# Running both score units of a key block back to back, with the AV output in the FFN's PSUM ring

## The chip, the cores and the metric

The kernel runs on one core of a Trainium2 chip. The metric is the device time of one execution in microseconds (us); each version was executed several times, and medians are given. A run can contain stretches of 3.4 us in which TensorE gets half its clock.

Names: PE is TensorE, DVE is VectorE, ACT is ScalarE, POOL is GpSimd. The kernel uses PSUM, where TensorE writes its results, as eight banks of 128 x 512 fp32 values.

## The reference, cut to what matters

Attention with a sliding window and four sink tokens, then RMS normalisation and a SwiGLU FFN:

```python
scores = scale * np.matmul(q, k.transpose(0, 1, 3, 2))       # q, k, v: 4 x 8 heads x 768 x 64
keep = is_sink | in_window                                   # 4 sinks, window of 128
a = softmax(np.where(keep, scores, -1e9))
x = (a @ v) transposed to 3072 x 512
xn = x / rms(x) * rms_g
g, val = xn @ w_gate, xn @ w_val                             # 512 -> 1536
out = (g * sigmoid(g) * val) @ w_out                         # 1536 -> 512, fp32
```

The kernel cuts the 3072 rows into 24 key blocks of 128 and, for the FFN, into 6 groups of 4 blocks.

## The kernel before

TensorE executes in the order of the program text. ScalarE's and VectorE's order in the main part is chosen at build time. All semaphores are made automatically: a tile taken from a pool waits until the last reader of the tile that had that buffer before is done. Tiles of one tag form a ring: with `bufs=4`, most tiles wait for the one four tiles earlier. (Which bank a tile gets is fixed at build time. In the kernel after, rebuilt to check this, about three reuses in four are at that distance; the others are from two to seven tiles back.)

The PSUM banks of the main part: four for the tag `b1` (gate `pg`, value `pvl`, output `po`, transposes `pqk` and `pxt`, sink tiles `pss` and `pvs`), two for `pT` (one slot of two banks), two for `pv`.

```python
# ... (pools)
pp[0] = ctx.enter_context(tc.tile_pool(name="psum", bufs=4, space=bass.MemoryType.PSUM))

def unit_s(g, u):                    # scores of 4 heads of key block g
    # ...
    pT = pp[0].tile([P, 2, 512], FP32, name="pT", tag="pT", bufs=1)
    for j in range(2):
        hp = 2 * u + j
        for hi in range(2):
            pr = slice(hi * D, (hi + 1) * D)         # 64 of the 128 rows of the array
            nc.tensor.matmul(out=pT[:, hi, j * 256:j * 256 + w],
                lhsT=QKT[b][pr, 1, hp, t * P:(t + 1) * P],
                rhs=QKT[b][pr, 0, hp, t * P:t * P + w], start=True, stop=True)      # L366
    et = epool.tile([P, 4, 2, P], BF16, name="et")
    nc.scalar.activation(out=et[...], in_=pT[...], func=ACT.Exp, scale=inv_sqrt_d)  # L373
    # ... mask: one DVE product (L386), or two POOL selects for later blocks (L388, L393)

def unit_av(g, u):                   # A times V of 4 heads, with the softmax sum as 65th column
    pv = pp[0].tile([P, 512], FP32, name="pv", tag="b1" if PROLOGUE[0] else "pv", bufs=2)
    # ... 4 to 9 short matmuls, then reciprocal (L449) and scaling (L454) on DVE,
    # sum of squares on ACT (L464); after u == 1 the normalisation chain on DVE (L473 to L511)

def parts_f(G, fts, cols):           # two parts of the FFN: gate and value
    def gate():                      # 4 matmuls of 512 columns into pg, then
        # ... th = tanh(pg / 2) on ACT (L564)
    def val():                       # 4 matmuls into pvl, then
        # ... p1 = (th + 1) * pg on DVE (L569): pg's bank is free
        # ... hT = p1 * pvl on DVE (L577): pvl's bank is free
# parts_o: 12 matmuls into po in three parts (L592), then osb = po / 2 on ACT (L599), DMA out

def step(g):                         # the attention work of block g in four slots
    slots = [[], [], [], []]
    if g < NB:
        slots[0].append(lambda: unit_s(g, 0))
        slots[2].append(lambda: unit_s(g, 1))
        # ... sink units in slot 1
    if g <= NB:
        slots[1].append(lambda: unit_av(g - 1, 0))
        slots[3].append(lambda: unit_av(g - 1, 1))
    # ... transposes of x in slot 0, of q and k in slots 1 or 2
    return slots
# weave(): the slots are spread evenly between the FFN's parts
```

The softmax here doesn't subtract the row's maximum and nothing guards it: scores larger than these inputs give would overflow.

## Time and profile before

| | before |
|---|---|
| time, median of 4 runs beside the change | 262.55 us (262.2 to 262.65) |
| TensorE busy | 93% |
| VectorE, ScalarE, GpSimd busy | 68%, 53%, 37% |
| TensorE waits of the profiled run after 38 us | 4.2 us |

These are lines of the page of the kernel before: busy time and share, then the span in 40 slices of 6.6 us (a digit is the busy share in tenths), the clock that TensorE was granted, and the chain of work that ended last.

```profile
...
PE 244.9 (93%) x1735; PEld 125.7 (48%) x1762; DVE 178.9 (68%) x471; ACT 137.9 (53%) x277; POOL 98.4 (37%) x131
...
PE   5878969989999999999999997999999999999994
...
DVE  3566866798768999438899449799338894078800
...
PEclk9999997999999999999999999999999999999998
...
PE 76%; DMA 10%; ACT 4%; DVE 4%; POOL 3%; issue 2%; POOLq 0%; ACTq 0%
...
```

From the seventh slice on TensorE has nine tenths or more almost everywhere: it is the limit, and 76% of the chain is its work. But VectorE has stretches of 8s and 9s too (the ninth, the thirteenth to the sixteenth, and so on): these are the gate/value stretches of the FFN groups. There is little room behind TensorE.

From the groups view, the three large groups of matmuls. After the bar: busy us, mean ns of one, then the us for which TensorE sat idle just before them, and for whom.

```profile
...
L551 PE MATMUL pg<-xnt,wg 128*128 128x512 bf16 (+1 forms) x321 | 74.4, 356 | 2.6 <-DVE p_2594 L569 1.7
L551 PE MATMUL pvl<-xnt,wv 128*128 128x512 bf16 (+1 forms) x319 | 74.0, 356 | 0.9 <-ACT xnt L537 0.5
L592 PE MATMUL po<-wo,hT 128*128 128x512 bf16 x278 | 65.7, 379 | 0.5
...
```

And from the waits view of TensorE: who waited for whom, us in total, times, longest.

```profile
...
PE pg L551 <- DVE p_2594 L569: 1.7, 1, 1.7
PE pT L366 <- ACT qkT L263: 1.4, 2, 0.9
PE pT L366 <- ACT qkT L241: 1.3, 2, 0.7
...
PE pvl L551 <- ACT xnt L537: 0.5, 1, 0.5
...
```

Past the start-up there is one long wait: 1.7 us, a gate tile whose bank was held until VectorE's product L569 was done. No line has a score unit waiting for an exponential to free `pT`.

The timeline of TensorE around one score unit shows why one wants to bring the two units together (start us, length us, line, count; the length runs to the modelled end of the last matmul):

```profile
...
102.26 1.03 PE L551 MATMUL pvl<-xnt,wv 128*128 128x512 bf16 x4
103.22 0.39 PE L366 MATMUL pT<-qkT 64*128 64x256 bf16 x4
103.54 1.90 PE L592 MATMUL po<-wo,hT 128*128 128x512 bf16 x8
...
```

Gate and value matmuls of 512 columns follow each other every 0.216 us. Four value matmuls started at 102.26 make the next start due at 103.12. The score unit starts at 103.22, 0.10 us late. The output matmul comes 0.32 us after it. The two matmuls of a pair use different halves of the rows and run together (they start 3 to 4 ns apart), so the visit is two pairs of 256 columns. The Trainium skill ("TensorEngine Tiling (Array Packing)", Key Properties) says that a change of tiling mode drains TensorE; this trace agrees.

### The profile page before, as it was taken

What the parts mean: (1) busy time and instruction counts of PE and PEld (TensorE: products, weight loads), DVE (VectorE), ACT (ScalarE), POOL (GpSimd) and SP (SyncE); (2) the same over time, 40 slices, a digit from 0 to 9 for tenths busy, and PEclk for the clock granted to TensorE, in tenths of its full rate; (3) what the DMA queues carried; (4) which work ended last, traced back from release to release, by engine and by line L of the source; (5) the groups of instructions that cost most, each with busy time, mean ns of one, the idle gap of its engine ahead of it and who ended that gap; (6) DMA issues with size and microseconds to landing.
All of it is one profiled execution on the core that took longest, in us unless ns stands there. A gap on an engine that the chain in (4) does not pass through costs nothing.

```text
span 262.4 us, 4760 instructions
## 1 busy us (share of the span) xinstructions
PE 244.9 (93%) x1735; PEld 125.7 (48%) x1762; DVE 178.9 (68%) x471; ACT 137.9 (53%) x277; POOL 98.4 (37%) x131
## 2 busy tenths in 40 slices
PE   5878969989999999999999997999999999999994
PEld 2446757845454444444454443444444454444441
DVE  3566866798768999438899449799338894078800
ACT  2646755687786546456465554464654542233211
POOL 8997679299988340413112001114112000000000
PEclk9999997999999999999999999999999999999998
DMA  9999999999999999441112450411330112300022
GB/s 98 138 173 182 187 163 186 185 155 149 170 178 181 147 134 130 105 149 30 22 21 42 116 148 16 62 21 40 102 101 1 22 20 60 114 8 0 0 82 80
DMA packets 105991, 25.74 MB, mean 98 GB/s; under 512 B 95088, under 2 KB 102768, under 8 KB 105968
## 3 DMA queue, kind: packets, MB, share of 16 engines
q0 software_dynamic: 82784, 14.16, 75.5%
q1 hardware_dynamic: 23184, 11.28, 18.8%
q8 instruction: 14, 0.23, 0.4%
q14 instruction: 9, 0.07, 0.1%
HBM read 28.57 MB, written 6.29 MB: 133 GB/s over the span
## 4 chain that ended last, share of the span: by engine, by line
PE 76%; DMA 10%; ACT 4%; DVE 4%; POOL 3%; issue 2%; POOLq 0%; ACTq 0%
PE pg L551 22%; PE pvl L551 21%; PE po L592 21%; PE pT L366 4%; DMA qs<-in_q_dram 4%; DMA wg<-in_moe_w_gate_dram 3%; DMA wv<-in_moe_w_val_dram 3%; PE pv L426 2%; ACT et L373 1%; PE pv L422 1%; PE pqk L228 1%; PE pv L414 1%; PE pss L298 1%; POOL qs L111 1%; ACT sq L464 1%
## 5 line engine op out<-in xcount | busy, mean ns | idle before, releaser
L551 PE MATMUL pg<-xnt,wg 128*128 128x512 bf16 (+1 forms) x321 | 74.4, 356 | 2.6 <-DVE p_2594 L569 1.7
L551 PE MATMUL pvl<-xnt,wv 128*128 128x512 bf16 (+1 forms) x319 | 74.0, 356 | 0.9 <-ACT xnt L537 0.5
L592 PE MATMUL po<-wo,hT 128*128 128x512 bf16 x278 | 65.7, 379 | 0.5
L564 ACT ACTIVATE th<-pg 128x512 bf16<-128x512 f32 x72 | 42.7, 594 | 42.1 <-PE pg L551 41.4
L388 POOL TENSOR_SCALAR_AFFINE_SELECT et<-et 128x512 bf16<-128x512 bf16 x20 | 12.8, 638 | 87.2 <-ACT et L373 71.7
L373 ACT ACTIVATE et<-pT 128x1024 bf16<-128x1024 f32 (+1 forms) x42 | 39.4, 937 | 10.2 <-PE pT L366 10.2
L551 PEld LDWEIGHTS <-wv 128*128 128x128 bf16 x328 | 30.5, 99 | 28.2 <-issue 2.3
L551 PEld LDWEIGHTS <-wg 128*128 128x128 bf16 x328 | 30.1, 98 | 28.6 <-issue 4.0
L592 PEld LDWEIGHTS <-hT 128*128 128x128 bf16 x288 | 26.4, 98 | 29.5 <-issue 1.5
L599 ACT ACTIVATE osb<-po 128x512 f32<-128x512 f32 x24 | 14.3, 595 | 28.3 <-PE po L592 24.3
L111 POOL DMA_DIRECT2D qs<-in_q_dram x24 | 21.5, 897 | 9.3 <-DMA wo<-in_moe_w_out_dram 2.6
L111 POOL DMA_DIRECT2D ks<-in_k_dram x24 | 21.4, 892 | 7.8 <-PE pg L551 2.7
L449 DVE RECIPROCAL rden<-pv 128x4 f32<-128x4 f32 x48 | 8.4, 176 | 19.7 <-PE pv L426 19.7
L366 PE MATMUL pT<-qkT 64*128 64x256 bf16 (+1 forms) x168 | 15.8, 267 | 2.9 <-ACT qkT L263 1.4
L386 DVE TENSOR_TENSOR et<-et,masks 128x1024 bf16<-128x1024 bf16 (+1 forms) x22 | 14.1, 640 | 5.7 <-ACT et L373 5.5
L366 PEld LDWEIGHTS <-qkT 64*128 64x128 bf16 x168 | 5.3, 94 | 18.7 <-issue 18.3
L426 PEld LDWEIGHTS <-et 128*128 128x128 bf16 x168 | 11.6, 97 | 1.6
L422 PEld LDWEIGHTS <-et 128*128 128x128 bf16 x136 | 10.8, 98 | 3.1
L393 POOL TENSOR_SCALAR_AFFINE_SELECT et<-et 128x512 bf16<-128x512 bf16 x16 | 11.1, 692 | 0.0
L414 PE MATMUL pv<-vsk,esk 128*128 128x260 bf16 x32 | 8.8, 274 | 0.0
L263 ACT COPY qkT<-pqk 128x1024 bf16<-128x1024 bf16 x8 | 8.1, 1007 | 0.9 <-PE pqk L228 0.9
L228 PE MATMUL pqk<-ident,qs 128*128 128x128 bf16 x56 | 5.5, 221 | 2.8 <-DMA qs<-in_q_dram 2.8
(318 smaller groups left out, 341.8 us busy)
## 6 DMA issues: line engine op xcount, KB each, us to landing
out_dram<-osb SPq DMA_DIRECT2D x24, 256.0 KB, 2.2
qs<-in_q_dram POOLq DMA_DIRECT2D x24, 128.0 KB, 7.4
ks<-in_k_dram POOLq DMA_DIRECT2D x24, 128.0 KB, 7.5
wg<-in_moe_w_gate_dram POOLq DMA_DIRECT2D x6, 256.0 KB, 7.6
wv<-in_moe_w_val_dram POOLq DMA_DIRECT2D x6, 256.0 KB, 8.0
wo<-in_moe_w_out_dram POOLq DMA_DIRECT2D x2, 768.0 KB, 11.0
v_100<-in_v_dram POOLq DMA_DIRECT2D x6, 128.0 KB, 7.8
v_102<-in_v_dram POOLq DMA_DIRECT2D x6, 128.0 KB, 7.7
```

Source lines behind the costliest of these rows:

```text
L111: nc.gpsimd.dma_start(out=tl, in_=src[b, :, t * P:(t + 1) * P, :].rearrange("h t d -> t h d"),)
L366: nc.tensor.matmul(out=pT[:, hi, j * 256:j * 256 + w], lhsT=QKT[b][pr, 1, hp, t * P:(t + 1) * P], rhs=QKT[b][pr, 0, hp, t * P:t * P + w], ...
L373: nc.scalar.activation(out=et[:, :, 0:nq, :].rearrange("p x n c -> p x (n c)"), in_=pT.rearrange("p i (j c) -> p (i j) c", c=256)[:, :, 0: ...
L386: nc.vector.tensor_tensor(out=ev, in0=ev, in1=mv, op=ALU.mult)
L388: nc.gpsimd.affine_select(out=et[:, :, 0, :], in_=et[:, :, 0, :], compare_op=ALU.is_ge, fill=0.0, base=0, pattern=[[0, 4], [1, P]], channe ...
L414: nc.tensor.matmul(out=pv[:, 0:HW], lhsT=ESK[(b, t)], rhs=VSK[b][:, 4 * u:4 * u + 4, :], start=True, stop=False, skip_group_check=True,)
L422: nc.tensor.matmul(out=dest, lhsT=E[(g - 1, h, 1)], rhs=V16[b][:, t - 1, h, :], start=(t == 1), stop=False, skip_group_check=True,)
L426: nc.tensor.matmul(out=dest, lhsT=E[(g, h, 0)], rhs=V16[b][:, t, h, :], start=(t == 0), stop=True, skip_group_check=True,)
L551: nc.tensor.matmul(out=ps[:, i * n:(i + 1) * n], lhsT=w_sb[:, kt, ft * P:(ft + 1) * P], rhs=XNT[G][:, kt, cols], start=(kt == 0), stop=(kt ...
L564: nc.scalar.activation(out=st["th"], in_=st["pg"], func=ACT.Tanh, scale=0.5)
L592: nc.tensor.matmul(out=st["po"], lhsT=HT[(G, ft // 2)][:, ft % 2, tb * P:(tb + 1) * P], rhs=wo[:, ft, :], start=(ft == 0), stop=(ft == FTN ...
L599: nc.scalar.mul(osb, st["po"], 0.5)
```

## The change

The intent: run the two score units of a block as one visit of eight matmuls. Each needs its own PSUM slot then, or the second would wait for the exponential of the first. The second slot takes two banks, and these are the two that AV had; AV goes into the ring of four with everything else. The diff, cut to its core:

```diff
@@ unit_bias, unit_s
-        pT = pp[0].tile([P, 2, 512], FP32, name="pT", tag="pT", bufs=1)
+        pT = pp[0].tile([P, 2, 512], FP32, name="pT", tag="pT", bufs=2)
@@ unit_av
-            [P, 512], FP32, name="pv", tag="b1" if PROLOGUE[0] else "pv", bufs=2
+            [P, 512], FP32, name="pv", tag="b1"
@@ step
             slots[0].append(lambda: unit_s(g, 0))
-            slots[2].append(lambda: unit_s(g, 1))
+            slots[0].append(lambda: unit_s(g, 1))
...
-            slots[0].append(lambda: unit_x(g - 3))
+            slots[0].insert(0, lambda: unit_x(g - 3))
@@ (the first two unit_x are taken out of their slots, as before)
-        slots[6].pop()
-        slots[10].pop()
+        slots[6].pop(0)
+        slots[10].pop(0)
```

The step function makes blocks 5 to 23, so 19 blocks are paired.

More of the change, by code (lines that the diff above doesn't have):

```diff
@@ L360, in unit_s @@
         w = nq * P
-        pT = pp[0].tile([P, 2, 512], FP32, name="pT", tag="pT", bufs=1)
+        pT = pp[0].tile([P, 2, 512], FP32, name="pT", tag="pT", bufs=2)
         for j in range(2):
```

## The prediction

> **What bounds it now.** Up to about 38 us the kernel waits for loads (slice view: DMA 9 of ten). From there TensorE is the limit: it is 93% busy over the span, and the chain of waits is 76% PE, 10% DMA, 4% ACT, 4% DVE. The groups view shows few PE waits: 2.6 us before pg, 0.9 before pvl, 2.9 before pT. A second limit lies close behind: in the gate/value stretches the windows view has VectorE busy 94% (78-103 us), 88% (118-142) and 86% (154-181), and the longest late wait, 1.68 us at 162 us, is a gate matmul whose bank waits for VectorE's product (L569).
>
> **What the change saves.** Score units use 64 rows of the array, their neighbours 128. The Trainium skill ("TensorEngine Tiling (Array Packing)", Key Properties) says that a change of tiling mode drains TensorE. The timeline agrees: value matmuls start every 0.216 us from 102.26, so the next start is due at 103.12; the score unit starts at 103.22 (0.10 late), and the next matmul 0.32 us after it, though two pairs of 256 columns need 0.213. A visit costs about 0.21 us beyond its work. In 19 blocks (5 to 23) two visits become one: at most 19 x 0.21 = 4.0 us. The second pT slot itself saves almost nothing: the waits view has no PE wait for an exponential (L373) to free pT.
>
> **What it costs.** Two AV tiles a block join the ring of four banks that holds gate, value, output, transposes and sink tiles. pg is free only after tanh (0.59 us) and product (0.66), pvl after another 0.69, pv after reciprocal and scaling (0.17 + 0.42), each behind queues. I laid the recorded bank releases against the tile order with AV included: if releases stay put while TensorE slips, 2 to 3.5 us of stalls appear; if they slip along entirely, 13. Tightest: 58-74 us, where units come at every part and an output tile's bank waits for its scaled copy (L599) behind exponentials and copies; then 125-139, 162 and 174 us, where VectorE is behind. Estimate between: 4 us.
>
> The two exponentials (1.02 us each) now come together, so a tanh behind them is up to 1 us later; in blocks below 12 the two mask products (0.68 each) come together too. Where an AV tile is among the next three ring tiles, this reaches the gate bank: estimate 0.5 us. And where VectorE is full, perhaps 0.5 us of TensorE's saving is lost.
>
> **Sum.** Gain 4.0; costs 4 + 0.5 + 0.5 = 5. All lies past 38 us on the critical path. Net +1 us: **263.5 us**, 8 times in 10 between 259.2 and 268.5. Faster by over 2%: 0.05; within 2%: 0.78; slower by over 2%: 0.17.
>
> **What the profile would show.** Right: pT matmuls in runs of eight, with one entry gap of 0.10 us and one exit of 0.11 a block; new PE waits before pg, pvl, po and pv, on VectorE (L569, L577, L454) and ScalarE (L599), 4-6 us more than before, most at 55-78 us and in the late gate/value stretches; no new wait before pT; start-up and the last stretch (from 217 us) unchanged in length. Wrong: no new waits, then about 258.6 us; or waits over 9 us, then slower by over 2%.
>
> **What would make it wrong.** ScalarE's and VectorE's order is chosen anew at build time: it may put tanh and products ahead of exponentials and masks, and hide the stalls; or put normalisation late, so that AV tiles hold ring banks long. Adjacency may also not remove the drain.

## The result

| | before | after |
|---|---|---|
| median of 4 runs | 262.55 us | 265.89 us (265.06 to 266.77) |
| ratio | | 1.013, 95% interval 1.0093 to 1.0167 |
| profiled span | 262.4 us | 265.1 us |

A ratio here is the mean time of one kernel's runs over the mean of the other's of the same rounds, so it is not quite the ratio of the medians. The change is 1.3% slower: a loss clear of noise, but under 2%.

The same lines of the page, after:

```profile
...
PE 243.9 (92%) x1735; PEld 128.9 (49%) x1762; DVE 181.7 (69%) x471; ACT 138.1 (52%) x277; POOL 99.8 (38%) x131
...
PE   5978979978999989998999996999999999999994
...
DVE  3567868887779999439988459689329994078700
...
PEclk9999999999999999999999999799999999999999
...
PE 65%; DVE 14%; DMA 7%; POOL 6%; ACT 4%; issue 3%; POOLq 0%; ACTq 0%
...
```

TensorE's busy time fell by 1 us and the span grew by 2.7: time went into waiting. The chain shows it best: PE's share falls from 76 to 65%, VectorE's rises from 4 to 14%. VectorE's own busy share is almost what it was (69% instead of 68), with the same 471 instructions. It is waited for more, without having more to do.

The groups:

```profile
...
L551 PE MATMUL pvl<-xnt,wv 128*128 128x512 bf16 (+1 forms) x322 | 74.3, 356 | 3.3 <-DVE p L569 1.4
L551 PE MATMUL pg<-xnt,wg 128*128 128x512 bf16 (+1 forms) x317 | 74.4, 355 | 2.1 <-DVE hT L577 0.9
...
L592 PE MATMUL po<-wo,hT 128*128 128x512 bf16 x279 | 65.0, 379 | 1.1 <-DVE p L569 0.6
...
```

The idle time before value matmuls rises from 0.9 to 3.3 us and before output matmuls from 0.5 to 1.1; the AV group, which had none but a 1.0 us wait for a load at the start, now has a wait of 1.9 us. The waits view lists them (only those past the start-up are shown, and the one of `pT` for comparison):

```profile
...
PE pv L426 <- DVE p L569: 1.9, 1, 1.9
...
PE pvl L551 <- DVE p L569: 1.4, 2, 0.9
PE pT L366 <- ACT qkT L241: 1.3, 2, 0.7
...
PE pvl L551 <- DVE y L479: 0.9, 1, 0.9
PE pg L551 <- DVE hT L577: 0.9, 2, 0.7
PE pvl L551 <- DVE hT L577: 0.8, 2, 0.5
PE po L592 <- DVE p L569: 0.6, 1, 0.6
...
PE pqk L228 <- ACT osb L599: 0.3, 1, 0.3
...
```

Each line but that of `pT` is a tile that waits for a bank: for a gate product (L569), a value product (L577), an output copy (L599). "DVE y L479" names the wrong instruction: that value tile, at 58.76 us, has the bank of a sink tile, whose reader L287 ran from 58.28 to 58.70. Added over the trace past 38 us, TensorE's waits are 8.8 us, against 4.2 before; the waits for banks alone are 6.8 us against 2.2 (the gate tile's 1.7 and a value tile's 0.5, whose bank the copy L537 still read). The longest is not new: the 1.9 us of AV at 164 us wait for the same kind of product as the gate tile's 1.7 us, at the same place, in the kernel before. These idle times are still too small: the profile lets a 512-column matmul last 0.38 us while the next could start after 0.216, so each wait after such a matmul hides another 0.16 us.

One such wait in full. This is the timeline of the kernel after, on all engines, with other rows left out (start, length, engine, line, count, and in brackets idle time and releaser):

```profile
...
120.30 1.03 PE L551 MATMUL pvl<-xnt,wv 128*128 128x512 bf16 x4
...
121.26 0.61 PE L366 MATMUL pT<-qkT 64*128 64x256 bf16 x8
...
121.69 1.94 ACT L373 ACTIVATE et<-pT 128x1024 bf16<-128x1024 f32 x2 [0.18 <-PE pT L366]
...
121.80 1.04 PE L551 MATMUL pg<-xnt,wg 128*128 128x512 bf16 x4
...
122.68 1.03 PE L551 MATMUL pvl<-xnt,wv 128*128 128x512 bf16 x4
...
123.52 0.60 ACT L564 ACTIVATE th<-pg 128x512 bf16<-128x512 f32 x1
...
123.89 1.02 PE L551 MATMUL pg<-xnt,wg 128*128 128x512 bf16 x3
...
124.07 1.08 DVE L511 SCALAR_TENSOR_TENSOR xr<-x,y,gb 128x512 bf16<-128x512 bf16 x1
...
125.07 0.68 DVE L569 SCALAR_TENSOR_TENSOR p<-th,pg 128x512 bf16<-128x512 bf16 x1
...
125.80 1.02 PE L551 MATMUL pvl<-xnt,wv 128*128 128x512 bf16 x4 [0.89 <-DVE p L569]
...
```

The gain is there: value matmuls from 120.30, next start due at 121.16, eight score matmuls at 121.26, next matmul at 121.80. That is 0.10 + 0.54 us for a block, where two visits before cost 2 x (0.10 + 0.32) = 0.84: 0.20 us saved.

Then it is given back. The gate tile at 121.80 ends at 122.84. Its tanh starts at 123.52, because ScalarE has both exponentials to do first (1.94 us). Its product L569 starts only at 125.07, because VectorE's order has the block's normalisation chain ahead of it, with `xr` (L511) from 124.07 to 125.15 last. So its bank is free at 125.75. The ring since then: gate (121.80), value (122.68), AV (between 123.5 and 123.9), gate (123.89), and now the value tile that needs the first one's bank. It should start at 124.75 and starts at 125.80. Without the AV tile in the ring, the tile that reuses this bank would be the one after, due at 125.6: by this reckoning a wait of about 0.2 us instead of 1.05.

### The profile page after: what moved, and what is told of

Read it like the earlier page. It is cut to its first block, busy times and chain, and to the rows that moved or that the text cites. A ratio compares the mean times of both kernels' runs of the same rounds, so it can differ in the third digit from the quotient of the medians.

```text
span 265.1 us, 4754 instructions
## 1 busy us (share of the span) xinstructions
PE 243.9 (92%) x1735; PEld 128.9 (49%) x1762; DVE 181.7 (69%) x471; ACT 138.1 (52%) x277; POOL 99.8 (38%) x131
## 4 chain that ended last, share of the span: by engine, by line
PE 65%; DVE 14%; DMA 7%; POOL 6%; ACT 4%; issue 3%; POOLq 0%; ACTq 0%
PE po L592 23%; PE pg L551 18%; PE pvl L551 16%; DMA qs<-in_q_dram 4%; DVE p L569 4%; DMA wg<-in_moe_w_gate_dram 3%; DVE hT L577 3%; DVE xr L511 3%; PE pT L366 2%; ACT th L564 2%; POOL v L124 2%; DVE et L386 2%; ACT et L373 1%; PE pqk L228 1%; PE pv L426 1%
## 5 line engine op out<-in xcount | busy, mean ns | idle before, releaser
L564 ACT ACTIVATE th<-pg 128x512 bf16<-128x512 f32 x72 | 42.8, 595 | 51.5 <-PE pg L551 51.4
L569 DVE SCALAR_TENSOR_TENSOR p<-th,pg 128x512 bf16<-128x512 bf16 x72 | 49.2, 684 | 24.3 <-ACT th L564 23.8
L577 DVE TENSOR_TENSOR hT<-p,pvl 128x512 bf16<-128x512 bf16 x72 | 49.3, 685 | 3.9 <-DVE p L569 0.5
L388 POOL TENSOR_SCALAR_AFFINE_SELECT et<-et 128x512 bf16<-128x512 bf16 x20 | 12.6, 636 | 84.7 <-ACT et L373 62.8
L373 ACT ACTIVATE et<-pT 128x1024 bf16<-128x1024 f32 (+1 forms) x42 | 37.7, 942 | 5.7 <-PE pT L366 5.7
L464 ACT ACTIVATE sq<-x 128x256 bf16<-128x256 bf16 x48 | 19.9, 415 | 20.0 <-DVE x L454 19.7
L599 ACT ACTIVATE osb<-po 128x512 f32<-128x512 f32 x24 | 14.3, 598 | 28.1 <-PE po L592 22.4
L124 POOL DMA_DIRECT2D v<-in_v_dram x24 | 21.4, 893 | 1.7 <-DMA qs<-in_q_dram 1.0
L511 DVE SCALAR_TENSOR_TENSOR xr<-x,y,gb 128x512 bf16<-128x512 bf16 (+1 forms) x25 | 20.6, 827 | 0.6
L454 DVE TENSOR_TENSOR x<-pv,rden 128x256 bf16<-128x256 f32 x48 | 20.2, 422 | 1.0
L426 PE MATMUL pv<-v,et 128*128 128x65 bf16 x168 | 15.3, 193 | 1.9 <-DVE p L569 1.9
L386 DVE TENSOR_TENSOR et<-et,masks 128x1024 bf16<-128x1024 bf16 (+1 forms) x22 | 13.9, 639 | 3.4 <-ACT et L373 3.2
L366 PE MATMUL pT<-qkT 64*128 64x256 bf16 (+1 forms) x168 | 12.3, 262 | 1.3 <-ACT qkT L241 1.3
```

The costliest lines, as they stand in the source:

```text
L124: nc.gpsimd.dma_start(out=V16[b][:, t, :, 0:D], in_=v[b, :, t * P:(t + 1) * P, :].rearrange("h t d -> t h d"),)
L373: nc.scalar.activation(out=et[:, :, 0:nq, :].rearrange("p x n c -> p x (n c)"), in_=pT.rearrange("p i (j c) -> p (i j) c", c=256)[:, :, 0: ...
L386: nc.vector.tensor_tensor(out=ev, in0=ev, in1=mv, op=ALU.mult)
L454: nc.vector.tensor_tensor(out=X16[g][:, heads_of(g, u), :], in0=pvv[:, :, 0:D], in1=RDEN.pop((g, u)).unsqueeze(2).to_broadcast((P, 4, D)), ...
L464: nc.scalar.activation(out=sq, in_=xh, func=ACT.Square, scale=MS_SCALE, accum_out=MS[g][:, u:u + 1],)
L511: nc.vector.scalar_tensor_tensor(out=XR[g][-1], in0=x16[:, c], scalar=y[:, 4:5], in1=gb[:, c], op0=ALU.mult, op1=ALU.mult,)
```

## The experiments

Twelve runs were made, of correct kernels unless said. An estimate from the reference's inputs: q and k are 0.1 times normal numbers, so scaled scores are about 0.01, softmax is nearly flat, and exchanged scores hardly change the output. The theories when they began: **A**, a ring of four is too shallow with AV in it; **B**, what costs is that exponentials and masks now come together; **C**, VectorE is full, and what TensorE gains does not count.

### 1. Sharing alone: share_only

```diff
 (kernel before)
-            [P, 512], FP32, name="pv", tag="b1" if PROLOGUE[0] else "pv", bufs=2
+            [P, 512], FP32, name="pv", tag="b1"
```

> The kernel before, with one edit: AV tiles (pv) take the ring of four banks (b1) instead of two of their own; score units stay apart, one pT slot. Theory A (the ring of four is too shallow once AV is in it; pairing itself gains 3 to 3.5 us): all of the cost and none of the gain, so 267.5 to 269.5 us, with 6 to 7 us of new PE waits before pg, pvl, po, pv. Theory B (the two exponentials and masks that now come together delay tanh and products; sharing is harmless): within 0.7 us of before, 262 to 263.3. Theory C (VectorE is full, so nothing gained on TensorE counts): says nothing of sharing by itself, about 263 to 266.

Measured: 265.88 us beside 264.2 for the kernel before; ratio 1.0069 (1.0027 to 1.0111). Sharing costs something, about 1.8 us, but much less than A said. Two of the long waits of after are already here (0.8 us before a value tile at 125 us, 1.8 us before AV at 164 us); those at 88, 97, 135, 176 and 205 us are not.

### 2. Sharing with depth: share_ring6

```diff
 (share_only)
-            tc.tile_pool(name="psum", bufs=4, space=bass.MemoryType.PSUM)
+            tc.tile_pool(name="psum", bufs=6, space=bass.MemoryType.PSUM)
```

> As share_only, but the shared ring has six banks (the same eight banks in all as the kernel before: pT 2, ring 6). Theory A: depth is what counts, so the waits go and the time is that of before or a little less, 261.5 to 262.8 us. If mixing AV with the FFN in one order of allocation is what hurts, whatever the depth, it stays near share_only, 266 or more.

Measured: ratio 0.9937 (0.9898 to 0.9975). With the same eight banks as the kernel before, but AV in one ring of six, the kernel is a little faster than before. Mixing AV with the FFN does no harm; the depth of the ring is what counts.

### 3. Pairing alone: pair_free

```diff
 (kernel after; wrong result on purpose)
-            [P, 512], FP32, name="pv", tag="b1"
+            [P, 512], FP32, name="pv", tag="b1" if PROLOGUE[0] else "pv", bufs=2
+    def unit_s2(g):
+        pT = pp[0].tile([P, 2, 512], FP32, name="pT", tag="pT", bufs=1)
+        unit_s_mm(g, 0, pT)          # both units write into the same two banks,
+        unit_s_mm(g, 1, pT)          # one over the other,
+        unit_s(g, 0, pT)             # and both exponentials read them
+        unit_s(g, 1, pT)
@@ step
-            slots[0].append(lambda: unit_s(g, 0))
-            slots[0].append(lambda: unit_s(g, 1))
+            slots[0].append(lambda: unit_s2(g))
```

> Wrong result on purpose. Pairing without sharing: as the kernel after, but pv has its two own banks again, and the second score unit writes over the first in the one pT slot, so that eight score matmuls run back to back and both exponentials follow together, with no second slot needed. Theory A: the drain alone is gained, 262.5 less about 3.3: 258.8 to 259.7 us. Theory B: the bunched exponentials cost what the change cost, 264.5 to 266.5. Theory C: VectorE's load takes the gain, 261.5 to 262.8.

Measured: ratio 0.9818 (0.9781 to 0.9855), 4.8 us faster by that ratio. The pairing is worth what it promised and more. B and C fall in their plain form: the exponentials come together here too, and VectorE has the same work.

### 4. One ring of eight: ring8

```diff
 (kernel after)
-            tc.tile_pool(name="psum", bufs=4, space=bass.MemoryType.PSUM)
+            tc.tile_pool(name="psum", bufs=8, space=bass.MemoryType.PSUM)
@@ unit_bias
-            pT = pp[0].tile([P, 2, 512], FP32, name="pT", tag="pT", bufs=2)
-            banks = [pT[:, hi, :] for hi in range(2)]
+            banks = [pp[0].tile([P, 512], FP32, name="pT", tag="b1")
+                     for hi in range(2)]
@@ unit_s
-        pT = pp[0].tile([P, 2, 512], FP32, name="pT", tag="pT", bufs=2)
+        pT = [pp[0].tile([P, 512], FP32, name="pT", tag="b1") for hi in range(2)]
...
-        nc.scalar.activation(out=..., in_=pT[...], func=ACT.Exp, scale=inv_sqrt_d)
+        for hi in range(2):          # one exponential for each bank
+            nc.scalar.activation(
+                out=et[:, 2 * hi:2 * hi + 2, 0:nq, :].rearrange("p x n c -> p x (n c)"),
+                in_=pT[hi].rearrange("p (j c) -> p j c", c=256)[:, :, 0:w],
+                func=ACT.Exp, scale=inv_sqrt_d)
```

> A version meant to beat both: as the kernel after, but all eight banks are one ring of single banks; a score unit takes two of them, and its exponential is split in two of 512 columns (about 0.58 us each instead of 1.02 for 1024). A block takes about 14 tiles from 8 banks, where after takes 10 from 4. Theory A: pairing is kept and the waits go, 258.7 to 260.5 us. Theory B: bunching stays and ScalarE has 0.3 us a block more to do, 265 to 268. Theory C: 261.5 to 263.

Measured: 257.31 us, ratio 0.9758 (0.9722 to 0.9794). It is correct and beats both kernels, and by more than A expected. The groups view of ring8 shows the waits before the three large groups almost gone:

```profile
...
L552 PE MATMUL pg<-xnt,wg 128*128 128x512 bf16 (+1 forms) x328 | 74.1, 353 | 0.5 <-ACT xnt L538 0.5
L552 PE MATMUL pvl<-xnt,wv 128*128 128x512 bf16 (+1 forms) x328 | 74.1, 353 | 0.2 <-DVE p L570 0.2
L593 PE MATMUL po<-wo,hT 128*128 128x512 bf16 x288 | 66.3, 379 | 0.0
...
```

ScalarE's work rose from 138.1 us (after) to 139.5 for the split exponentials; no wait of TensorE is put down to an exponential.

### 5. The kernel after again: after_again

> The kernel after, unchanged, so that it stands in one call with the next three. Measured first at 1.013 of before; expected again 1.009 to 1.017. The profiled runs so far differ by one stretch of 3.4 us at half clock, which came in some runs and not in others: the runs with a mean clock of 0.999 should be 1 to 1.5 us shorter than those at 0.993, in every kernel.

Measured: ratio 1.0101 (1.0053 to 1.0149). The two runs with a mean clock of 0.992 took 266.48 and 266.61 us, the two at 0.999 and above 265.11 and 265.38: the half-clock stretch goes with 1.1 to 1.5 us.

### 6. Exponentials apart, first try: after_spread

```diff
 (kernel after)
-            slots[0].append(lambda: unit_s(g, 0))
-            slots[0].append(lambda: unit_s(g, 1))
+            slots[0].append(lambda: unit_s_mm(g, 0))     # unit_s cut in two:
+            slots[0].append(lambda: unit_s_mm(g, 1))     # matmuls, and exponential with mask
+            slots[0].append(lambda: unit_s_exp(g, 0))
+            slots[2].append(lambda: unit_s_exp(g, 1))
```

> As the kernel after (eight score matmuls back to back, two pT slots, AV in the ring of four), but the exponential and mask of the second unit are issued two slots later, where they stood in the kernel before. share_only showed that sharing alone costs only about 2 us, and pair_free that pairing alone gains about 5, so theory A alone (depth) does not add up to the +3.4 of after. Theory A2: the two interact, since the bunched exponentials delay tanh and so the freeing of gate banks, which only a shallow ring turns into PE waits. Then this is 3 to 5 us faster than after, 0.995 to 1.003 of before. If depth alone counts, it is within 1 us of after.

Measured: ratio 1.0037 (0.9983 to 1.0091). This run does not test what it was made for. In its trace the two exponentials still stand together in every block from 71 us on: ScalarE's order is chosen at build time, and it put them there again. What did move is on VectorE: at 96 us the second mask product no longer stands ahead of the value product, and the wait there (97 us in after) shrinks from 0.70 to 0.10 us. Moving a line in the program text does not move an instruction on an engine whose order is not yours.

### 7. The trick checked, at depth four: pair_share4

```diff
 (pair_free; wrong result on purpose)
-            [P, 512], FP32, name="pv", tag="b1" if PROLOGUE[0] else "pv", bufs=2
+            [P, 512], FP32, name="pv", tag="b1"
```

> Wrong result on purpose: pair_free (both score units into one pT slot, one over the other) with AV in the ring of four. It differs from the kernel after in the second slot alone, so it should be within 1 us of it; this shows that the trick of pair_free does not itself make the time. About 4 to 7 us above pair_free.

Measured: 266.81 us, ratio 1.0139 (1.0098 to 1.018), beside 1.0101 for after. Without the second slot it behaves as after does, so pair_free's time is not made by its trick.

### 8. The same at depth six: pair_share6

```diff
 (pair_share4; wrong result on purpose)
-            tc.tile_pool(name="psum", bufs=4, space=bass.MemoryType.PSUM)
+            tc.tile_pool(name="psum", bufs=6, space=bass.MemoryType.PSUM)
```

> Wrong result on purpose: pair_share4 with a shared ring of six banks. Theory A and A2: with the depth back the waits go, within 1 us of pair_free (0.982 of before) or a little under it. If AV's place in the order of allocation is what hurts, near pair_share4.

Measured: 257.07 us, ratio 0.9766 (0.9727 to 0.9805). Two banks more in the ring are worth 9.7 us between these two kernels, which differ in that one number. (By their mean clocks all four runs of pair_share4 have the half-clock stretch and none of pair_share6 has it, so some 1.3 us of this may be the clock's.) ScalarE's and VectorE's order is chosen anew at build time, but it hardly differs: by the two traces the order is the same on TensorE and GpSimd, for all but 4 of ScalarE's 277 instructions, and for all but 7 of VectorE's 471.

The same block as in the timeline of after, in pair_share6 (L364, L386, L564, L577, L524, L582 are here the scores, the exponential, gate and value, tanh, `xr` and the product):

```profile
...
118.00 0.61 PE L364 MATMUL pT<-qkT 64*128 64x256 bf16 x8
...
118.54 1.04 PE L564 MATMUL pg<-xnt,wg 128*128 128x512 bf16 x4
118.65 1.94 ACT L386 ACTIVATE et<-pT 128x1024 bf16<-128x1024 f32 x2 [0.40 <-PE pT L364]
...
119.41 1.03 PE L564 MATMUL pvl<-xnt,wv 128*128 128x512 bf16 x4
...
120.47 0.60 ACT L577 ACTIVATE th<-pg 128x512 bf16<-128x512 f32 x1
...
120.63 1.03 PE L564 MATMUL pg<-xnt,wg 128*128 128x512 bf16 x4
...
121.01 1.08 DVE L524 SCALAR_TENSOR_TENSOR xr<-x,y,gb 128x512 bf16<-128x512 bf16 x1
...
121.49 1.03 PE L564 MATMUL pvl<-xnt,wv 128*128 128x512 bf16 x4
...
122.11 0.65 DVE L582 SCALAR_TENSOR_TENSOR p<-th,pg 128x512 bf16<-128x512 bf16 x1
...
```

ScalarE and VectorE do the same things in the same order: both exponentials, then the tanh (2.5 us after the scores began, in after 2.3), then `xr`, then the product at 122.11, which again is late. But the value tile starts at 121.49, when it is due, although the gate tile's bank is not free until 122.76. It takes the bank of the gate tile six tiles earlier (the program's bank numbers say so), whose product had ended at 118.55. What makes this wait is not that the product is late, but that the ring has no bank to give while it is.

### 9. Exponentials apart, forced: after_late

```diff
 (after_spread)
+    def late(g, u):                  # queue unit 1's exponential behind the latest tanh
+        if u == 1 and g >= GB + 1 and "th" in LAST:
+            return tc.issue_after(LAST["th"])
+        return nullcontext()
...
-        nc.scalar.activation(out=..., func=ACT.Exp, ...)
+        with late(g, u):
+            nc.scalar.activation(out=..., func=ACT.Exp, ...)
```

> after_spread did not test what it was meant to: ScalarE's order, chosen at build time, kept both exponentials together from about 55 us on. Here the order is forced: the second unit's exponential is queued behind the latest tanh, and the compiled order shows it two gates later; the eight score matmuls stay together, and AV stays in the ring of four. Theory A2 (bunched exponentials delay tanh, and only a shallow ring turns that into PE waits): about 3 us under after (1.010 of before), so 0.997 to 1.003, and the waits at 97, 135, 176 and 205 us of after shrink or go. If depth alone makes the cost, within 1 us of after.

Measured: ratio 1.004 (0.999 to 1.009). Here the trace has the exponentials apart in most blocks from 76 us on. By the ratios that is 0.6% less than after_again, with intervals that overlap, and no less than after_spread (1.0037), whose exponentials stood together. Of the waits named in advance, the one at 97 us shrinks from 0.70 to 0.10 us, but it did so in after_spread too; that at 205 us shrinks from 0.54 to 0.14; those at 135 and 176 us grow, from 0.34 to 0.43 and from 0.45 to 1.04. One not named, at 125 us, shrinks from 0.89 to 0.55. So bunched exponentials lengthen some waits, but that they cost time over the whole kernel is not shown, and with them apart most of the cost remains.

### 10. Eight banks without pairing: ring8_apart

```diff
 (ring8)
             slots[0].append(lambda: unit_s(g, 0))
-            slots[0].append(lambda: unit_s(g, 1))
+            slots[2].append(lambda: unit_s(g, 1))
```

> ring8 with the score units apart again, two slots from each other as in the kernel before. The pairing's gain at a depth at which banks do not bind: ring8 was 0.9758 of before; with 0.18 us a block for 19 blocks lost (3.4 us), this should be 0.986 to 0.991. If it is as fast as ring8, the gain of ring8 was of depth alone and pairing is worth nothing.

Measured: ratio 0.9927 (0.9871 to 0.9983). The median run is a little slower than expected; pairing is worth 1.7% at this depth.

### 11. VectorE's chain moved: after_rms

```diff
 (kernel after)
-        if u == 1 and g >= 2:
+        if u == 1 and 2 <= g < GB:
             unit_rms(g)
...
+    def behind_p(g):                 # two slots later, and behind the latest product L569
+        with tc.issue_after(LAST["p"]):
+            unit_rms(g)
...
+        if GB <= g - 2 < NB:
+            slots[1].append(lambda: behind_p(g - 2))
```

> As the kernel after, but VectorE's normalisation chain of a block (six small instructions and xr, together 2 to 2.5 us) is issued two slots later and queued behind the latest gate product, instead of right after the second AV tile. In the traces of after and after_late this chain stood ahead of a product whose tanh was done, and held its gate bank about 1 us (at 124 to 125 us). Theory A3 (what the shallow ring cannot bear is any burst ahead of the products, on either engine): 1 to 2.5 us under after, 1.000 to 1.006 of before. If only depth counts, no change, or the waits merely move to other tiles: within 0.7 us of after.

Measured: ratio 1.0109 (1.007 to 1.0148): no gain. The waits at 97, 125, 135 and 205 us are gone, and others have come at 102, 109, 139, 178 us, and one of 2.5 us at 58 us, where transposes now wait for a later `xr`.

### 12. Both moves: after_late_rms

The two edits above together.

> Both moves at once: the second exponential queued behind a later tanh (after_late) and the chain queued behind a product (after_rms). Theory A3: the two add up, 3 to 4.5 us under after, 0.993 to 1.000 of before; the wait at about 125 us goes. If only depth counts: as after_late, 1.003 to 1.005. It should stay well above ring8 (0.976) under every theory, since the ring is still four deep.

Measured: ratio 1.009 (1.0036 to 1.0145). Theory A3 falls: the two do not add up. With a ring of four, rearranging who comes first on the other engines moves the waits about and takes away little.

### The runs in one table

The whole-kernel ratios to the kernel before, and in brackets the time from the first gate weight load of the second FFN group to the first output load of the fifth, taken from the timelines (about 78 to 217 us; none of these windows has a half-clock stretch, and start-up and tail are left out):

| banks | units apart | units paired |
|---|---|---|
| ring 4, AV has 2 of its own | before: 1 (138.6 us) | pair_free: 0.9818 (135.5 us) |
| ring 4 with AV | share_only: 1.0069 (140.0 us) | after_again: 1.0101 (140.05 us) |
| ring 6 with AV | share_ring6: 0.9937 (137.7 us) | pair_share6: 0.9766 (134.0 us) |
| ring 8 with AV and scores | ring8_apart: 0.9927 (137.0 us) | ring8: 0.9758 (133.75 us) |

In three rows pairing takes 3.1 to 3.7 us off this stretch. In the second it takes nothing off: TensorE arrives at the next wait earlier by what it saved, and waits that much longer (its idle times in this stretch are 2.6 us in share_only and 4.8 in after_again). In the first three rows the paired kernel also has the transposes of x ahead of the scores in their slot (the `insert` of the diff); in the last both have it, and pairing is worth as much there, so that edit is not what makes the difference. after_spread, after_late, after_rms and after_late_rms have 139.5, 139.3, 138.8 and 139.1 us here, so the rearrangements win back about 1 us of this stretch. Before it, from the first gate weights at about 39 us, after_rms and after_late_rms take 41.2 and 39.5 us, where after takes 38.8. after_rms has two half-clock stretches there, which can account for its 2.4 us by themselves; the other two have none.

## Why the prediction was right, and where its sizes were off

It gave 263.5 us with a range of 259.2 to 268.5, and within 2% as the likeliest. Measured: 265.89 us, 1.3% slower. The mechanism was the right one; two terms of the sum were off. The range was wide: a gain of 1% would have lain in it as well. And 4 us of stalls was picked between 2 and 13 with nothing in the trace to fix it, so that it came near is partly luck.

- **What bounds it.** Right: TensorE first, with VectorE close behind in the gate/value stretches. The chain of after goes through VectorE for 14% instead of 4%.
- **The gain, 19 x 0.21 = 4.0 us.** About right: the timeline shows 0.20 us a block, and pair_free is 4.8 us faster by its ratio. A part of the difference would be the two waits for the q/k copy L263 in the kernel before, together 1.4 us, which are gone in pair_free.
- **No saving from the second slot itself, no new wait before `pT`.** Right: the idle time before `pT` matmuls went from 2.9 to 1.3 us, and none of it waits for an exponential.
- **The cost, "4 + 0.5 + 0.5 = 5".** This is the term that was too small. Between pair_free and after_again, two profiled runs of equal mean clock (0.991 and 0.992), lie 258.1 and 264.8 us: 6.7 us. By the ratios it is 1.0101 - 0.9818 = 2.8%, or 7.4 us. So the net was about +3 and not +1.
- **What makes it up.** The prediction added stalls of the ring, and 0.5 us for the bunching, as separate costs. The runs show that sharing and pairing do not add: sharing alone costs 0.7%, pairing alone gains 1.8%, and together they cost 1.0 to 1.4%. Why the estimate missed this is argued and not shown: it laid the bank releases of the *old* trace against the new order, and could not say how far the same releases come later relative to TensorE once TensorE has less to do between them.
- **"Where VectorE is full, perhaps 0.5 us of TensorE's saving is lost."** Not seen as such: with six or eight banks the saving is there in full, with VectorE at 71%. With four banks that AV shares all of it is lost in the steady stretch. It is the depth that decides, not VectorE's load by itself.
- **Waits 4 to 6 us more, on L569, L577, L454 and L599.** 4.6 us more by the idle times, all of it waits for banks, on L569, L577, L599 and, not named, L287. One more wait of 0.16 us is hidden in most of them. A wait for L454, AV's scaling, is not among the releasers shown. The places at 55 to 78, 125 to 139, 162 and 174 us were right; those at 88, 97 and 205 us had not been named.
- **Start-up and the last stretch unchanged.** Right: the start-up's last wait ends at 38.0 us before and 38.4 after, and from the first output load of the fifth group to the end both kernels take 45.6 us.
- **What would make it wrong.** ScalarE's new order did not hide the stalls; it put both exponentials ahead of the tanh.

What stays open is how much of the cost each late instruction has. after_late, after_rms and after_late_rms show that no single one has most of it, and their intervals overlap that of after.

### The clock

The clock lines of the two pages have a 7 each, in different slices. In the profiled run of before the clock record shows TensorE at half clock from 38.8 us for 3.413 us, after waits of 1.4 and 0.7 us at the end of the start-up. In the profiled run of after there is no such stretch there, but one from 166.0 us, 1.4 us after the wait of 1.9 us ended; it makes that run's fourth group 29.0 us long, where after_again, with the same wait and no such stretch there, takes 27.3. The Trainium skill ("TensorE: Matmul & The Clock Gate", Part 1: The HAM clock gate) tells of two states, half and full, and of a free-running window of 3413 ns; the traces agree as to the states (1.0 and 0.5 alone occur) and the length (in before the half-clock stretch is 3.413 us, and the full-clock ones around it are 10 and 64 times as long, 34.133 and 218.453). A half-clock stretch goes with 1.1 to 1.7 us more, and whether a run has it differs from run to run of one kernel. That a wait brings it on is suggested by where these stretches stand, and not shown. Differences of under 1% between single runs are not to be read without looking at this.

## What to carry to other kernels

Count, for a ring of PSUM banks, how many tiles are allocated between a tile and its reuse, and compare the time of those with the longest delay of the tile's readers, queues included; a bank taken from a neighbour for a good purpose can cost more than the purpose gains. When two changes are made in one edit, measure them in a two-by-two table: here one gained 1.8%, the other cost 0.7%, and together they cost over 1%. And a pool cut into fixed parts can be worse than one ring of all the banks: the same eight banks as one ring turned a loss of 1% into a gain of 2.4%.

## What the Trainium skill lacked or had wrong

- "TensorEngine Tiling (Array Packing)", Key Properties, says that a mode switch drains TensorE, but not what that costs. Here, between 128-row and 64-row matmuls: about 0.10 us on the way in and as much on the way out.
- "TensorE: Matmul & The Clock Gate", Back-to-back issue gap, gives a sustained pace of about 131 ns for 512-column matmuls with weight loads between. The trace has 0.216 us, in stretches of dozens of load and matmul pairs; that is the page's figure for the isolated gap.
- The same page's rule (HAM oscillation) warns of idle gaps over about 3.4 us; of shorter ones it says only that frequent ones can throttle the clock, without a length. Here half-clock stretches followed waits of 1.9 us and shorter (38.8 us in before, 166.0 us in after), in some executions and not in others; that the waits brought them is not shown.
- "Perfetto Trace Analysis" (Identifying the Most-Contended Engine) names, beside the share of the peak FLOP rate, the busy share of weight loads as the better measure of how far one is from the roof. Between kernels this close the second misleads: it is 48% in before and 49% in after, which is slower, and 50% in ring8, which is the fastest.
- No page that was read tells how deep a ring of banks has to be for its readers' delays. Here 4, 6 and 8 banks with AV in the ring and paired scores gave 1.0101, 0.9766 and 0.9758 of the time before (the one with six with a wrong result).
